# Centring two row tiles ahead of their 1/std at the start of a fused attention and MLP kernel

## The chip, the cores and the metric

The kernel runs on one core of a Trainium2 chip. The metric is the device time of a launch in microseconds, as a median over runs; the kernel before takes 693.07 us. The span in a profile is some 1.7 to 2.0 us shorter, as it goes from the first to the last instruction. Each run also records the mean clock granted to TensorE.

Names used below: PE is TensorE's matmul side, PEld its weight loads, DVE is VectorE, ACT is ScalarE, SP is the engine that issues nearly all DMAs. A *row tile* is 128 of the 2048 rows; block 0 is row tiles 0 to 3. V(j,c) is the group of eight matmuls that makes columns half c of V for row tile j. "Q" is the first of the 128 matmuls that make Q and K of block 0.

## The reference, cut to what matters

```python
def _layernorm(x, axis=-1, eps=1e-5):
    m = jnp.mean(x, axis=axis, keepdims=True)
    v = jnp.var(x, axis=axis, keepdims=True)
    return (x - m) / jnp.sqrt(v + eps)
...
    x = A_x                                              # 1 x 2048 x 1024, bf16
    h = x + _A_ref(_layernorm(x, axis=-1), A_wqkv, A_wo) # sliding window attention, 32 heads
    h2 = h + _B_ref(_layernorm(h, axis=-1), B_w1, B_w2)  # silu MLP, F = 3584
```

V = layernorm(x) @ Wv. Division by the standard deviation is one number for each row, so it can be done after the matmul: V = ((x - mean) @ Wv) * (1/std). The change uses this for two row tiles.

## The kernel before

Layernormed rows must lie transposed (features on partitions) in `lnT_b[0]` before TensorE can use them. Tiles 0, 1 and 2 of block 0 are transposed by TensorE and copied out of PSUM by ScalarE; tile 3 by a DMA transpose. In the traces VectorE, ScalarE and TensorE's matmuls run in the order in which the program issues them.

```python
    load_x(0, 0)
    load_wqkv(2 * D)              # V weights, columns half 0: 1 MB
    load_x(0, 1, nc.scalar)
    load_x(0, 2)
    load_wqkv(2 * D + 512)        # V weights, columns half 1: 1 MB
    load_x(0, 3)
    load_wqkv(0)                  # first 512 columns of Q
    ...
    for i in range(11):           # warm-up of TensorE
        nc.tensor.matmul(o_ps[i % 2][:]..., lhsT=warm[:, 0, 0:P], rhs=warm[:, 0, :], start=True, stop=True)

    def turn_first(j, h):         # two transposes by TensorE, one copy by ScalarE
        for i in range(2):
            kt = h * 2 + i
            nc.tensor.transpose(out=tp_ps[h][:, i * P:(i + 1) * P], in_=x_ring[j][:, kt * P:(kt + 1) * P], identity=ident[:])
        nc.scalar.copy(out=lnT_b[0][:, h * 2:(h + 1) * 2, j * P:(j + 1) * P], in_=tp_ps[h][:, 0:256]...)
    ...
    ln_stats(x_ring[0], st, 0)                 # bn_stats x2, bn_aggr
    ln_root(st, rs, 0)                         # ScalarE sqrt
    ln_half(x_ring[1], half, 0)
    ln_first(x_ring[0], st, rs, 0, 4, 1)       # reciprocal, (x - mean) * rstd in 4 pieces
    ln_stats(x_ring[1], st, 1, half)
    for h in range(4):
        turn_first(0, h)
        ...
    v_group(0, 0, 0, lambda **args: held.append(args), turn_1)
    ...
    v_group(0, 1, 0, act, turn_1_rest)
    ln_first(x_ring[2], st, rs, 2, 1)
    ln_stats(x_ring[3], st, 3)
    ln_root(st, rs, 3)
    ln_first(x_ring[3], st, rs, 3, 1)
    ln_transpose(x_ring[3], lnT_b[0], 3)       # DMA transpose
    for c0 in (D, 512, D + 512):
        load_wqkv(c0)
    v_group(0, 0, 1, act)
    for h in range(4):
        turn_first(2, h)
    v_group(0, 1, 1, act)
    v_group(0, 2, 0, act)
    ...                                        # V(2,1), V(3,0), V(3,1), then Q and K
```

The softmax here doesn't subtract the row's maximum and nothing guards it: scores larger than these inputs give would overflow.

Of the kernel before, what the change touches and what calls it, by code (L numbers as in the profile page):

```python
# [9 lines left out]
F32 = mybir.dt.float32  # L10
I32 = mybir.dt.int32
ACT = mybir.ActivationFunctionType
ALU = mybir.AluOpType

P = 128
# [29 lines left out]
def kernel(  # L45
# [10 lines left out]
    nc = tc.nc  # L56
# [3 lines left out]
    S, D = x2d.shape  # L60
# [4 lines left out]
    KT = D // P  # L65
# [4 lines left out]
    scale = float(DH) ** -0.5  # L70

    const = ctx.enter_context(tc.tile_pool(name="const", bufs=1))
    small = ctx.enter_context(tc.tile_pool(name="small", bufs=2))
# [12 lines left out]
    r_e = big.tile([P, 13312], BF16, name="r_e")  # L86
# [4 lines left out]
    tp_ps = [tp_pool.tile([P, 1024], BF16, name=f"tp{i}") for i in range(4)]  # L91
    o_ps = [ps.tile([P, 8, 64], F32, name=f"o_ps{i}") for i in range(2)]
    acc_ps = [ps.tile([P, 512], F32, name=f"acc{i}") for i in range(2)]

    def view(region, off, *dims):
        n = 1
        for d in dims:
            n *= d
        ap = region[:, off:off + n]
        if len(dims) == 2:  # L100
            return ap.rearrange("p (a b) -> p a b", b=dims[1])
        if len(dims) == 3:
            return ap.rearrange("p (a b c) -> p a b c", b=dims[1], c=dims[2])
        return ap
# [4 lines left out]
    lnT_b = [view(r_w, 24576, KT, 512), view(r_t, 0, KT, 512)]  # L109
    x_ring = [view(r_o, i * 1024, 1024) for i in range(8)]  # L110
# [17 lines left out]
    wqkv_v = A_wqkv.rearrange("(kt p) n -> p kt n", p=P)  # L128
# [5 lines left out]
    def load_x(b, j, queue=nc.sync):  # L134
        queue.dma_start(out=x_ring[(b % 2) * 4 + j], in_=x2d[(b * 4 + j) * P:(b * 4 + j + 1) * P, :])  # L135

    def load_wqkv(c0):
        dst = wqk[:, :, c0:c0 + 512] if c0 < 2 * D else wv[:, :, c0 - 2 * D:c0 - 2 * D + 512]
        nc.sync.dma_start(out=dst, in_=wqkv_v[:, :, c0:c0 + 512])

    eps = const.tile([P, 1], F32, name="eps")
    nc.vector.memset(eps[:], LN_EPS)
# [1 line left out]
    nc.scalar.activation(out=dummy[:], in_=eps[:], func=ACT.Sqrt)  # L144

    load_x(0, 0)
    load_wqkv(2 * D)
    load_x(0, 1, nc.scalar)
    load_x(0, 2)
    load_wqkv(2 * D + 512)  # L150
    load_x(0, 3)
    load_wqkv(0)

    ident = const.tile([P, P], BF16, name="ident")
    make_identity(nc, ident[:])
    warm = view(r_e, 0, 2, 512)
    nc.vector.memset(warm, 0.0)
    nc.gpsimd.memset(v[:, :, :, DH:VW], 1.0)


    for i in range(11):
        nc.tensor.matmul(o_ps[i % 2][:].rearrange("p a b -> p (a b)"), lhsT=warm[:, 0, 0:P], rhs=warm[:, 0, :], start=True, stop=True)


    def ln_half(xt, stats, c):
        nc.vector.bn_stats(out=stats[:, c, :], in_=xt[:, c * 512:(c + 1) * 512])

    def ln_stats(xt, st, j, half_done=None):
        stats = half_done
        if stats is None:  # L170
            stats = small.tile([P, 2, 6], F32, name="ln_st", tag="ln_st")
            ln_half(xt, stats, 0)
        ln_half(xt, stats, 1)
        nc.vector.bn_aggr(out=st[:, j, :], in_=stats[:])
# [18 lines left out]
    def ln_norm(xt, st, rs, j):  # L193
        nc.vector.tensor_scalar(out=xt, in0=xt, scalar1=st[:, j, 0:1], scalar2=rs[:, j:j + 1],
                                op0=ALU.subtract, op1=ALU.mult)

    def ln_transpose(xt, dst, j):
        nc.sync.dma_start_transpose(out=dst[:, :, j * P:(j + 1) * P], in_=xt)

    def ln_root(st, rs, j):  # L200
        nc.scalar.activation(out=rs[:, j:j + 1], in_=st[:, j, 1:2], func=ACT.Sqrt, bias=eps[:], scale=1.0)

    def ln_first(xt, st, rs, j, parts, on_act=0):

        if on_act:
            shift = small.tile([P, 2], F32, name="ln_shift", tag="ln_shift")
            nc.scalar.activation(out=shift[:, 0:1], in_=st[:, j, 0:1], func=ACT.Identity, scale=-1.0)
        nc.vector.reciprocal(out=rs[:, j:j + 1], in_=rs[:, j:j + 1])
        if on_act:
            nc.scalar.activation(out=shift[:, 1:2], in_=shift[:, 0:1], func=ACT.Identity, scale=rs[:, j:j + 1])  # L210
        n = 1024 // parts
        for h in range(parts):
            part = xt[:, h * n:(h + 1) * n]
            if h < parts - on_act:
                ln_norm(part, st, rs, j)
            else:
                nc.scalar.activation(out=part, in_=part, func=ACT.Identity, bias=shift[:, 1:2], scale=rs[:, j:j + 1])

    def turn_first(j, h):

        for i in range(2):
            kt = h * 2 + i
            nc.tensor.transpose(out=tp_ps[h][:, i * P:(i + 1) * P], in_=x_ring[j][:, kt * P:(kt + 1) * P], identity=ident[:])  # L223
        nc.scalar.copy(out=lnT_b[0][:, h * 2:(h + 1) * 2, j * P:(j + 1) * P],
                       in_=tp_ps[h][:, 0:256].rearrange("p (k q) -> p k q", q=P))

    def ln_tiles(tag):
        st = small.tile([P, 4, 2], F32, name=f"st_{tag}", tag=f"st_{tag}")
        rs = small.tile([P, 4], F32, name=f"rs_{tag}", tag=f"rs_{tag}")
        return st, rs  # L230
# [3 lines left out]
    acc_banks = list(a[:] for a in acc_ps)  # L234

    def next_acc():
        acc_n[0] += 1
        return acc_banks[acc_n[0] % len(acc_banks)]

    def v_group(b, j, c, copy, between=None):  # L240
        acc = next_acc()
        for kt in range(KT):
            if between:
                between(kt)
            nc.tensor.matmul(acc, lhsT=lnT_b[b % 2][:, kt, j * P:(j + 1) * P], rhs=wv[:, kt, c * 512:(c + 1) * 512],  # L245
                             start=(kt == 0), stop=(kt == KT - 1))
        copy(out=v[:, b * 4 + j, c * 16:(c + 1) * 16, 0:DH], in_=acc.rearrange("p (h d) -> p h d", d=DH))
# [172 lines left out]
    class Stream:  # L420
# [18 lines left out]
        def between(self, kt):  # L439
            if self.seen * self.n >= self.done * 192:  # L440
                self.bursts[self.done]()
                self.done += 1
            if self.seen * self.n * 2 >= (self.given * 2 + 1) * 192:
                if pending:
                    pending.pop(0)()
                coming.append(self.pieces[self.given])
                if len(coming) > self.behind:
                    pending.append(coming.pop(0))
                self.given += 1
            self.seen += 1  # L450

    dve, act = nc.vector.tensor_copy, nc.scalar.copy


    st, rs = ln_tiles("a")
    half = small.tile([P, 2, 6], F32, name="ln_st", tag="ln_st")
    ln_stats(x_ring[0], st, 0)
    ln_root(st, rs, 0)
    ln_half(x_ring[1], half, 0)
    ln_first(x_ring[0], st, rs, 0, 4, 1)  # L460
    ln_stats(x_ring[1], st, 1, half)
    for h in range(4):
        turn_first(0, h)
        if h == 2:
            ln_root(st, rs, 1)
    ln_first(x_ring[1], st, rs, 1, 4)
    ln_stats(x_ring[2], st, 2)

    held = []

    def turn_1(kt):
        if kt == 7:
            turn_first(1, 0)

    def turn_1_rest(kt):
        if kt == 2:
            turn_first(1, 3)
            act(**held.pop())
            ln_root(st, rs, 2)

    v_group(0, 0, 0, lambda **args: held.append(args), turn_1)
    turn_first(1, 1)
    turn_first(1, 2)
    v_group(0, 1, 0, act, turn_1_rest)
    ln_first(x_ring[2], st, rs, 2, 1)
    ln_stats(x_ring[3], st, 3)
    ln_root(st, rs, 3)
    ln_first(x_ring[3], st, rs, 3, 1)
    ln_transpose(x_ring[3], lnT_b[0], 3)
    for c0 in (D, 512, D + 512):  # L490
        load_wqkv(c0)
    v_group(0, 0, 1, act)
    for h in range(4):
        turn_first(2, h)
    v_group(0, 1, 1, act)
    v_group(0, 2, 0, act)
    v_group(0, 2, 1, act)
    nc.scalar.activation(out=dummy[:], in_=eps[:], func=ACT.Exp)
    v_group(0, 3, 0, act)
    v_group(0, 3, 1, act)  # L500

    ps_tp.__exit__(None, None, None)
    ps_sc = tc.tile_pool(name="ps_sc", bufs=1, space=bass.MemoryType.PSUM, reuse_waits="tile")
# [28 lines left out]
    for g0 in range(0, G, 4):  # L532
        for w in range(2):
            for g in range(g0, g0 + 4):
                qk_group(0, w, g, dve if g % 2 else act)
                n = g0 * 2 + w * 4 + g % 4
# [105 lines left out]
    for b in range(NB):  # L642
# [4 lines left out]
        for ft in range(FT):  # L647
# [8 lines left out]
            if b == 0 and 6 <= ft < 14:  # L656
                j, c = divmod(ft - 6, 2)
# [60 lines left out]
```

## Time and profile before

| | before |
|---|---|
| time, median of 3 | 693.07 us (692.89 to 693.12) |
| PE busy | 677.0 us, 98% of the span |
| first V matmul | 7.92 us |
| V(2,0) starts | 15.92 us (worked out in the prediction) |
| Q starts | 22.82 us |

TensorE is busy from start to end, so an instruction of another engine counts only where TensorE waits for it. The change concerns the first 23 us alone; from Q on the two programs are the same.

### The profile page before, as it was taken

What the parts mean: (1) busy time and instruction counts of PE and PEld (TensorE: products, weight loads), DVE (VectorE), ACT (ScalarE), POOL (GpSimd) and SP (SyncE); (2) the same over time, 40 slices, a digit from 0 to 9 for tenths busy, and PEclk for the clock granted to TensorE, in tenths of its full rate; (3) what the DMA queues carried; (4) which work ended last, traced back from release to release, by engine and by line L of the source; (5) the groups of instructions that cost most, each with busy time, mean ns of one, the idle gap of its engine ahead of it and who ended that gap; (6) DMA issues with size and microseconds to landing.
All of it is one profiled execution on the core that took longest, in us unless ns stands there. A gap on an engine that the chain in (4) does not pass through costs nothing.

```text
span 691.4 us, 14107 instructions
## 1 busy us (share of the span) xinstructions
PE 677.0 (98%) x5895; PEld 331.6 (48%) x6011; DVE 290.5 (42%) x609; ACT 241.8 (35%) x463; POOL 160.4 (23%) x295
## 2 busy tenths in 40 slices
PE   8999999999999999999999999999999999999998
PEld 3444455555555555544444444444444444444445
DVE  5267646744444439534315133343133251333111
ACT  5326666766666666421310033300133100233000
POOL 1007666656666666500000000000000000000000
PEclk9999999999999999999999999999999999999999
DMA  8732242136241889971023410022300024100110
GB/s 251 251 55 78 39 80 61 26 63 183 73 131 17 241 235 281 213 277 50 12 80 111 93 39 0 1 91 69 85 0 1 17 95 95 39 1 1 30 39 24
DMA packets 76463, 60.95 MB, mean 88 GB/s; under 512 B 50288, under 2 KB 60528, under 8 KB 76400
## 3 DMA queue, kind: packets, MB, share of 16 engines
q1 hardware_dynamic: 76256, 59.78, 32.0%
q8 instruction: 47, 0.77, 0.5%
q10 hardware_dynamic: 144, 0.26, 0.1%
q14 instruction: 16, 0.13, 0.1%
HBM read 39.85 MB, written 8.39 MB: 70 GB/s over the span
## 4 chain that ended last, share of the span: by engine, by line
PE 97%; issue 1%; DMA 1%; SPq 0%; DVE 0%
PE hacc L628 19%; PE hacc L665 17%; PE acc L255 16%; PE acc L665 10%; PE acc L628 9%; PE acc L245 8%; PE acc L276 7%; PE o_ps L388 5%; PE sc L308 3%; PE hacc L276 1%; DMA r_w<-in_A_wqkv_dram 1%; PE sc L360 1%; PE sc L334 1%; PE tp L223 0%; SPq L135 0%
## 5 line engine op out<-in xcount | busy, mean ns | idle before, releaser
L378 POOL TENSOR_SCALAR_AFFINE_SELECT r_e<-r_e 128x512 bf16<-128x512 bf16 (+1 forms) x288 | 157.4, 561 | 126.6 <-ACT r_e L368 62.7
L665 PEld LDWEIGHTS <-r_a 128*128 128x128 bf16 x952 | 90.9, 98 | 103.0
L628 PEld LDWEIGHTS <-r_w 128*128 128x128 bf16 x896 | 87.4, 98 | 105.0 <-issue 0.2
L665 PE MATMUL hacc<-r_a 128*128 128x512 bf16 (+2 forms) x607 | 121.8, 359 | 0.5
L628 PE MATMUL hacc<-r_e,r_w 128*128 128x512 bf16 x444 | 99.7, 379 | 0.5
L320 ACT ACTIVATE r_e<-sc 128x768 bf16<-128x768 f32 x96 | 78.2, 814 | 48.3 <-PE sc L308 47.6
L637 ACT ACTIVATE r_n<-hacc 128x512 f32<-128x512 f32 x30 | 17.9, 597 | 178.9 <-PE hacc L628 175.5
L665 PE MATMUL acc<-r_a 128*128 128x512 bf16 x329 | 73.5, 379 | 0.4
L255 PEld LDWEIGHTS <-r_w 128*128 128x128 bf16 x512 | 44.2, 97 | 46.1 <-issue 1.0
L255 PE MATMUL acc<-r_t,r_w 128*128 128x512 bf16 x233 | 60.3, 379 | 2.4 <-issue 1.7
L257 DVE CAST r_a<-acc 128x512 bf16<-128x512 f32 x56 | 38.6, 690 | 56.6 <-PE acc L255 43.8
L255 PE MATMUL acc<-r_w 128*128 128x512 bf16 x240 | 58.0, 379 | 1.5 <-issue 0.9
L388 PEld LDWEIGHTS <-r_e 128*128 128x128 bf16 x1440 | 47.4, 96 | 17.9
L276 PE MATMUL acc<-r_o,r_a 128*128 128x512 bf16 x188 | 49.5, 379 | 1.9 <-issue 1.3
L628 PE MATMUL acc<-r_e,r_w 128*128 128x512 bf16 x213 | 48.9, 379 | 0.3
L388 PE MATMUL o_ps<-r_a,r_e 128*128 128x33 bf16 x1440 | 48.1, 178 | 0.1
L321 ACT ACTIVATE r_e<-sc 128x256 bf16<-128x256 f32 x96 | 37.6, 392 | 0.0
L680 DVE SCALAR_TENSOR_TENSOR r_t<-hacc,r_t 128x512 bf16<-128x512 f32 (+2 forms) x22 | 14.0, 635 | 55.2 <-PE hacc L665 53.8
L680 DVE SCALAR_TENSOR_TENSOR r_t<-acc,r_t 128x512 bf16<-128x512 f32 x12 | 8.3, 692 | 64.2 <-PE acc L665 58.8
L638 DVE SCALAR_TENSOR_TENSOR r_a<-r_n,hacc 128x512 bf16<-128x512 f32 x30 | 20.6, 688 | 33.0 <-ACT r_n L637 33.0
L628 PE MATMUL hacc<-r_a,r_w 128*128 128x512 bf16 x139 | 32.6, 379 | 0.3
L276 PEld LDWEIGHTS <-r_a 128*128 128x128 bf16 x256 | 21.8, 97 | 22.3
(79 smaller groups left out, 532.5 us busy)
## 6 DMA issues: line engine op xcount, KB each, us to landing
r_w<-in_B_w_dram SPq DMA_DIRECT2D x8, 896.0 KB, 5.2
r_a<-in_B_w_dram SPq DMA_DIRECT2D x7, 1024.0 KB, 7.5
r_w<-in_A_wqkv_dram SPq DMA_DIRECT2D x6, 1024.0 KB, 9.3
h_dram<-r_t SPq DMA_DIRECT2D x16, 256.0 KB, 2.5
r_t<-h_dram SPq DMA_DIRECT2D x16, 256.0 KB, 2.9
out_dram<-r_t SPq DMA_DIRECT2D x31, 128.0 KB, 1.7
r_o<-in_A_x_dram SPq DMA_DIRECT2D x15, 256.0 KB, 4.2
r_e<-h_dram SPq DMA_DIRECT2D x3, 1024.0 KB, 5.7
```

The costliest lines, as they stand in the source:

```text
L245: nc.tensor.matmul(acc, lhsT=lnT_b[b % 2][:, kt, j * P:(j + 1) * P], rhs=wv[:, kt, c * 512:(c + 1) * 512], start=(kt == 0), stop=(kt == KT ...
L255: nc.tensor.matmul(acc, lhsT=wqk[:, kt, col0:col0 + P], rhs=lnT_b[b % 2][:, kt, :], start=(kt == 0), stop=(kt == KT - 1))
L257: copy(out=(qT, kT)[which][b][:, g, :], in_=acc)
L276: nc.tensor.matmul(acc, lhsT=qT[b][:, g, j * P:(j + 1) * P], rhs=wo[:, g, c * 512:(c + 1) * 512], start=(g == 0), stop=(g == G - 1))
L308: nc.tensor.matmul(sc[hh // 2][half * 64:half * 64 + 64, hh % 2, col:col + qb - qa], lhsT=kT[t // 4][r0:r0 + DH, g, k0:k0 + 64], rhs=qT[b] ...
L320: nc.scalar.activation(out=tri[:, :, :, 64:256], in_=both, func=ACT.Exp, scale=scale)
L321: nc.scalar.activation(out=e[:, 1024:1280].rearrange("p (h q) -> p h q", q=P), in_=bank[:, :, 192:320], func=ACT.Exp, scale=scale)
L378: nc.gpsimd.affine_select(out=dst, in_=src, pattern=[[0, n] for n in dst.shape[1:-1]] + [[sgn, P]], compare_op=ALU.is_ge if upper else ALU ...
L388: nc.tensor.matmul(o_ps[pair][:, qt * 2 + hh, 0:VW], lhsT=chunk_of(i, bank, piece, pair, hh), rhs=v[:, b * 4 + kt, g * 4 + pair * 2 + hh, ...
L628: nc.tensor.matmul(acc, lhsT=w1[:, kt, ft * P:(ft + 1) * P], rhs=ln2T[b][:, kt, :], start=(kt == 0), stop=(kt == KT - 1))
L665: nc.tensor.matmul(acc[:, 0:c1 - c0], lhsT=gT[:, ft, j * P:(j + 1) * P], rhs=w2[ft // 4][:, ft % 4, c0:c1], start=(ft == 0), stop=(ft == F ...
L680: nc.vector.scalar_tensor_tensor(out=t_out[j % 2][:, c0:c1], in0=acc[:, 0:c1 - c0], scalar=0.5, in1=t_in[j % 2][:, c0:c1], op0=ALU.mult, o ...
```

## The change

Its intent is to let TensorE start sooner. Before, tile 0 had to have its mean, variance, root and reciprocal before it could be transposed. Now only its mean is made (half of it by a sum on ScalarE), the tile is centred and transposed, and 1/std follows when V is taken out of PSUM. Tile 1's mean is a sum on ScalarE. The V weights come in quarters and halves, so that the first matmuls can start on the first quarter. Tiles 0 and 1 must still be normalized in full for Q and K, which is done later, with two more DMA transposes. The warm-up of TensorE has ten matmuls instead of eleven and starts sooner, as VectorE clears less memory for it. The diff, cut (of the calls in its last part only the new ones are shown; those that they replace stand above):

```diff
     load_x(0, 0)
-    load_wqkv(2 * D)
-    load_x(0, 1, nc.scalar)
+    load_x(0, 1)
+    load_wqkv(2 * D, 4, (0, 3))
     load_x(0, 2)
-    load_wqkv(2 * D + 512)
+    load_wqkv(2 * D, 4, (3, 4))
+    load_wqkv(2 * D + 512, 2)
     load_x(0, 3)
     load_wqkv(0)
...
-    for i in range(11):
...
+    for i in range(10):
...
+    def mean_first():
+        nc.scalar.activation(out=scrap[:, 0:512], in_=x_ring[0][:, 512:1024], func=ACT.Identity, scale=-1.0 / D, accum_out=mean[:, 0:1])
+        ln_half(x_ring[0], half, 0)
+        nc.vector.tensor_scalar(out=mean[:, 1:2], in0=half[:, 0, 1:2], scalar1=half[:, 0, 4:5], scalar2=-0.25, op0=ALU.add, op1=ALU.mult)
+        nc.scalar.activation(out=scrap, in_=x_ring[1], func=ACT.Identity, scale=-1.0 / D, accum_out=mean[:, 2:3])
...
+    def scaled(j):                      # evacuation of a held V group, times 1/std of tile j
+        args = held.pop(0)
+        nc.scalar.activation(func=ACT.Identity, scale=rs[:, j:j + 1], **args)
...
+    mean_first()
+    center(0)
+    center(1)
+    turn_first(0, 0, x_mid[0])
+    turn_first(0, 1, x_mid[0])
+    v_group(0, 0, 0, hold, place({1: (0, 2), 3: (0, 3), 5: (1, 0), 6: (1, 1), 7: (1, 2)}))
+    turn_first(1, 3, x_mid[1])
+    ln_stats(x_ring[2], st, 2)
+    ln_root(st, rs, 2)
+    ln_stats(x_ring[0], st, 0, half)
+    ln_root(st, rs, 0)
+    ln_recip(rs, 2)
+    ln_norm(x_ring[2], st, rs, 2)
+    ln_recip(rs, 0)
+    v_group(0, 1, 0, hold)
+    v_group(0, 0, 1, hold)
+    scaled(0)
     ln_stats(x_ring[3], st, 3)
     ln_root(st, rs, 3)
+    ln_stats(x_ring[1], st, 1)
+    ln_root(st, rs, 1)
+    ln_recip(rs, 3)
+    ln_norm(x_ring[3], st, rs, 3)
     ln_transpose(x_ring[3], lnT_b[0], 3)
+    ln_recip(rs, 1)
+    scaled(1)
+    scaled(0)
+    v_group(0, 1, 1, hold)
+    for h in range(4):
+        turn_first(2, h, x_ring[2])
+    scaled(1)
+    for j in range(2):
+        ln_norm(x_ring[j], st, rs, j)
+        ln_transpose(x_ring[j], lnT_b[0], j)
     for c0 in (D, 512, D + 512):
         load_wqkv(c0)
```

While the V stage runs, four PSUM banks rotate instead of two, so that held groups can stay.

More of the change, by code (lines that the diff above doesn't have):

```diff
@@ L135, in load_x, with load_wqkv @@
         queue.dma_start(out=x_ring[(b % 2) * 4 + j], in_=x2d[(b * 4 + j) * P:(b * 4 + j + 1) * P, :])
-    def load_wqkv(c0):
+    def load_wqkv(c0, parts=1, some=None):
         dst = wqk[:, :, c0:c0 + 512] if c0 < 2 * D else wv[:, :, c0 - 2 * D:c0 - 2 * D + 512]
-        nc.sync.dma_start(out=dst, in_=wqkv_v[:, :, c0:c0 + 512])
+        n = KT // parts
+        for k in range(0, KT, n)[slice(*some or (0, parts))]:
+            nc.sync.dma_start(out=dst[:, k:k + n, :], in_=wqkv_v[:, k:k + n, c0:c0 + 512])
+    warm = view(r_e, 0, P)
+    nc.vector.memset(warm, 0.0)
     eps = const.tile([P, 1], F32, name="eps")
@@ L155 @@
     make_identity(nc, ident[:])
-    warm = view(r_e, 0, 2, 512)
-    nc.vector.memset(warm, 0.0)
     nc.gpsimd.memset(v[:, :, :, DH:VW], 1.0)
-    for i in range(11):
-        nc.tensor.matmul(o_ps[i % 2][:].rearrange("p a b -> p (a b)"), lhsT=warm[:, 0, 0:P], rhs=warm[:, 0, :], start=True, stop=True)
+    wide = bass.AP(tensor=warm.tensor, offset=warm.offset, ap=[warm.ap[0], [0, 4], warm.ap[1]])
+    for i in range(10):
+        nc.tensor.matmul(o_ps[i % 2][:].rearrange("p (a c) b -> p a (c b)", c=2), lhsT=warm, rhs=wide, start=True, stop=True)
     def ln_half(xt, stats, c):
@@ L201, in ln_root, with ln_recip, turn_first @@
         nc.scalar.activation(out=rs[:, j:j + 1], in_=st[:, j, 1:2], func=ACT.Sqrt, bias=eps[:], scale=1.0)
-    def ln_first(xt, st, rs, j, parts, on_act=0):
-        if on_act:
-            shift = small.tile([P, 2], F32, name="ln_shift", tag="ln_shift")
-            nc.scalar.activation(out=shift[:, 0:1], in_=st[:, j, 0:1], func=ACT.Identity, scale=-1.0)
+    def ln_recip(rs, j):
         nc.vector.reciprocal(out=rs[:, j:j + 1], in_=rs[:, j:j + 1])
-        if on_act:
-            nc.scalar.activation(out=shift[:, 1:2], in_=shift[:, 0:1], func=ACT.Identity, scale=rs[:, j:j + 1])
-        n = 1024 // parts
-        for h in range(parts):
-            part = xt[:, h * n:(h + 1) * n]
-            if h < parts - on_act:
-                ln_norm(part, st, rs, j)
-            else:
-                nc.scalar.activation(out=part, in_=part, func=ACT.Identity, bias=shift[:, 1:2], scale=rs[:, j:j + 1])
-    def turn_first(j, h):
+    def turn_first(j, h, src):
         for i in range(2):
             kt = h * 2 + i
-            nc.tensor.transpose(out=tp_ps[h][:, i * P:(i + 1) * P], in_=x_ring[j][:, kt * P:(kt + 1) * P], identity=ident[:])
+            nc.tensor.transpose(out=tp_ps[h][:, i * P:(i + 1) * P], in_=src[:, kt * P:(kt + 1) * P], identity=ident[:])
         nc.scalar.copy(out=lnT_b[0][:, h * 2:(h + 1) * 2, j * P:(j + 1) * P],
@@ L455 @@
     st, rs = ln_tiles("a")
-    half = small.tile([P, 2, 6], F32, name="ln_st", tag="ln_st")
-    ln_stats(x_ring[0], st, 0)
-    ln_root(st, rs, 0)
-    ln_half(x_ring[1], half, 0)
-    ln_first(x_ring[0], st, rs, 0, 4, 1)
-    ln_stats(x_ring[1], st, 1, half)
-    for h in range(4):
-        turn_first(0, h)
-        if h == 2:
-            ln_root(st, rs, 1)
-    ln_first(x_ring[1], st, rs, 1, 4)
-    ln_stats(x_ring[2], st, 2)
-    held = []
-    def turn_1(kt):
-        if kt == 7:
-            turn_first(1, 0)
@@ L475, in turn_1_rest @@
-    def turn_1_rest(kt):
-        if kt == 2:
-            turn_first(1, 3)
-            act(**held.pop())
-            ln_root(st, rs, 2)
-    v_group(0, 0, 0, lambda **args: held.append(args), turn_1)
-    turn_first(1, 1)
-    turn_first(1, 2)
-    v_group(0, 1, 0, act, turn_1_rest)
-    ln_first(x_ring[2], st, rs, 2, 1)
+    x_mid = [view(r_e, 1024 + 1024 * j, 1024) for j in range(2)]
+    scrap = view(r_e, 3072, 1024)
+    mean = small.tile([P, 3], F32, name="mean")
+    half = small.tile([P, 2, 6], F32, name="ln_half")
@@ new lines, in mean_first, with center @@
+    def mean_first():
[3 more added lines that the diff above has]
+        nc.scalar.activation(out=scrap, in_=x_ring[1], func=ACT.Identity, scale=-1.0 / D, accum_out=mean[:, 2:3])
+    def center(j):
+        for h in range(4):
+            out, in0 = (x[j][:, h * 256:(h + 1) * 256] for x in (x_mid, x_ring))
+            if j == 0:
+                nc.vector.tensor_scalar(out=out, in0=in0, scalar1=mean[:, 0:1], scalar2=mean[:, 1:2], op0=ALU.add, op1=ALU.add)
+            else:
+                nc.vector.tensor_scalar(out=out, in0=in0, scalar1=mean[:, 2:3], scalar2=None, op0=ALU.add)
@@ new lines, with hold, place @@
+    held = []
+    def hold(**args):
+        held.append(args)
+    def scaled(j):
+        args = held.pop(0)
+        nc.scalar.activation(func=ACT.Identity, scale=rs[:, j:j + 1], **args)
+    def place(at):
+        return lambda kt: turn_first(*at[kt], x_mid[at[kt][0]]) if kt in at else None
+    acc_banks += [o[:].rearrange("p a b -> p (a b)") for o in o_ps]
+    mean_first()
[4 more added lines that the diff above has]
+    v_group(0, 0, 0, hold, place({1: (0, 2), 3: (0, 3), 5: (1, 0), 6: (1, 1), 7: (1, 2)}))
@@ L486 @@
+    turn_first(1, 3, x_mid[1])
+    ln_stats(x_ring[2], st, 2)
+    ln_root(st, rs, 2)
+    ln_stats(x_ring[0], st, 0, half)
+    ln_root(st, rs, 0)
+    ln_recip(rs, 2)
[4 more added lines that the diff above has]
+    scaled(0)
     ln_stats(x_ring[3], st, 3)
     ln_root(st, rs, 3)
-    ln_first(x_ring[3], st, rs, 3, 1)
+    ln_stats(x_ring[1], st, 1)
+    ln_root(st, rs, 1)
+    ln_recip(rs, 3)
+    ln_norm(x_ring[3], st, rs, 3)
@@ L489 @@
     ln_transpose(x_ring[3], lnT_b[0], 3)
+    ln_recip(rs, 1)
+    scaled(1)
+    scaled(0)
+    v_group(0, 1, 1, hold)
+    for h in range(4):
+        turn_first(2, h, x_ring[2])
[3 more added lines that the diff above has]
+        ln_transpose(x_ring[j], lnT_b[0], j)
     for c0 in (D, 512, D + 512):
         load_wqkv(c0)
-    v_group(0, 0, 1, act)
-    for h in range(4):
-        turn_first(2, h)
-    v_group(0, 1, 1, act)
     v_group(0, 2, 0, act)
@@ L500 @@
     v_group(0, 3, 1, act)
+    del acc_banks[2:]
     ps_tp.__exit__(None, None, None)
```

## The prediction

> **What bounds the kernel now.** I began with the page: PE is 98% busy and carries 97% of the chain that ended last. TensorE therefore sets the end, and a change to the start counts only by the time at which TensorE gets through it.
>
> The diff touches nothing after the V stage of block 0, so I next read the chain of waits over the first 51 us (start, duration, what):
>
> ```profile
> 1.26 6.61 DMA r_w<-in_A_wqkv_dram
> 7.88 0.04 issue
> 7.92 1.67 PE acc L245 x7
> ...
> 13.90 0.45 PE tp L223 x8
> 14.35 8.63 PE acc L245 x40
> 22.98 0.22 PE acc L255
> ```
>
> The first V matmul waits for its 1 MB of V weights (7.87 us). From there PE hardly stops until the Q groups (L255). The 40 matmuls are the five groups V(1,1), V(2,0), V(2,1), V(3,0), V(3,1), written (row tile, column half). One group is 8 x 8.63/40 = 1.73 us. The timeline gives the same run by its starts, 14.19, with the first Q matmul at 22.82, so V(2,0) starts at 14.19 + 1.73 = 15.92. Behind V(2,0) lie 32 matmuls, 6.90 us, up to Q. My measure of the change is when V(2,0) starts in it.
>
> The issues by window give what can feed it, in order of issue from 1.7 to 5.5 us (the last figure is us from issue to landing; the windows overlap, so each line is one transfer):
>
> ```profile
> r_o<-in_A_x_dram SPq DMA_DIRECT2D x1, 256.0 KB, 6.8
> ...
> r_w<-in_A_wqkv_dram SPq DMA_DIRECT2D x1, 1024.0 KB, 9.2
> ...
> r_o<-in_A_x_dram SPq DMA_DIRECT2D x1, 256.0 KB, 9.0
> ...
> r_w<-in_A_wqkv_dram SPq DMA_DIRECT2D x1, 1024.0 KB, 9.8
> ```
>
> With the issue times 1.72, 2.35, 3.29 and 5.43 these land at 8.5 (x tile 2), 11.55 (V half 1), 12.3 (x tile 3) and 15.2 us (Q). Tiles 0 and 1 land at 0.81 + 3.4 = 4.2 and 0.97 + 3.9 = 4.9. From 7.87 to 15.2 us 2.62 MB came: 358 GB/s, a full stream.
>
> VectorE's timeline shows what tile 3 costs once it is there:
>
> ```profile
> 12.67 1.28 DVE L166 BATCH_NORM_STATS2 ln_st<-r_o 128x6 f32<-128x512 bf16 x2
> 13.98 0.21 DVE L174 BATCH_NORM_AGGREGATE st_a<-ln_st 128x2 f32<-128x12 f32 x1
> 14.55 0.16 DVE L208 RECIPROCAL rs_a<-rs_a 128x1 f32<-128x1 f32 x1 [0.36 <-ACT rs_a L201]
> 14.75 0.55 DVE L194 TENSOR_SCALAR r_o<-r_o,st_a,rs_a 128x1024 bf16<-128x1024 bf16 x1
> ```
>
> From statistics to statistics is 1.31 + 0.13 = 1.44 us (elsewhere the next one starts 0.13 after an aggregate), a reciprocal to a norm 0.20, a norm to the next instruction 0.46.
>
> The groups kept apart by shape give ScalarE's prices (mean ns after the busy us):
>
> ```profile
> L342 ACT ACTIVATE r_e<-sc 128x1024 bf16<-128x1024 f32 x24 | 23.3, 1021 | 10.5 <-PE sc L334 10.5
> L257 ACT CAST r_a<-acc 128x512 bf16<-128x512 f32 x8 | 4.7, 585 | 21.2 <-PE acc L255 21.2
> L224 ACT COPY r_w<-tp 128x256 bf16<-128x256 bf16 x12 | 3.8, 375 | 1.2 <-PE tp L223 1.2
> L217 ACT ACTIVATE r_o<-r_o,ln_shift,rs_a 128x256 bf16<-128x256 bf16 x1 | 0.6, 601 | 0.0
> ```
>
> **What the Trainium skill says.** "TensorE: Matmul & The Clock Gate", in the section on the array's architecture (16 sub-arrays of 32x32), calls ScalarE and VectorE strict FIFO: an instruction that waits holds back all behind it. The trace agrees: both run this stage in program order, and the reciprocal above kept a ready VectorE idle for 0.36 us. "DMA: Bandwidth & Descriptors", Queues, rings and completion order, says that descriptors of one ring are consumed in order; the landings above are in order of issue. "ScalarE: Activation LUTs", What ACT_TABLE_LOAD costs, gives 93 ns for each pointer operand; here two of them took a 256 column operation from 375 to 601 ns, 113 each. The clock gate page's Part 1 says that an idle window of about 3.4 us halves TensorE's clock, and that as long a busy one restores it. The warm-up, 11 matmuls in 4.87 us (443 ns each), against 216 in the V stage shows the two rates; no idle stretch here shows the fall.
>
> **The change, part by part.**
>
> *Loads.* Before x tile 3 the queue carries the same bytes (x 0 to 2, both V halves); they are only cut finer, and x tile 1 moves off ScalarE's queue. At about 0.7 us per 256 KB the quarters of V half 0 land (estimates) near 5.6, 6.3 and 7.0, and the last, behind x tile 2, near 8.4. V half 1 stays at 11.55, x tile 3 at 12.3, Q at 15.2.
>
> *The start.* Removed before the first transpose: half of tile 0's statistics, aggregate, root, reciprocal, shift. What stays is one half's statistics on VectorE (4.25 to 4.89) beside a sum of the other on ScalarE (0.6 and an accumulator read that I put at 0.2), one small operation, and centring in four pieces. The first piece is ready near 5.45 instead of 6.84. ScalarE then sums the whole of tile 1, about 1.0 + 0.2 us, ahead of the first copy, so that copy runs at 6.1 (7.34 before) and V(0,0) starts near 6.5. Its last two k steps wait for the fourth quarter: it ends near 8.95, tile 1's last transposes at 9.05. V(1,0) takes until 10.8, V(0,1) until 12.5 (its second half needs 11.55 and starts at 11.65), V(1,1) until 14.3, tile 2's transposes until 14.7. The same work is done at 15.92 now: PE is 1.2 us ahead.
>
> *What V(2,0) waits for.* Tile 2's four copies from PSUM stand on ScalarE behind two scaled evacuations, V(1,0) by tile 1's 1/std and V(0,1). The first needs reciprocal 1, which on VectorE stands behind statistics 3, statistics 1, reciprocal 3 and norm 3. Tile 1's statistics are work that used to be done by 8.1 us; now they follow x tile 3. Added up from 12.35: statistics 3, 1.44, is 13.79; statistics 1, 1.31 to its aggregate and 0.13, is 15.23; reciprocal 3, 0.20, is 15.43; norm 3, 0.46, is 15.89; reciprocal 1, 0.16 and the step to ScalarE (0.24 from its start, as at 6.26 to 6.50), is 16.13. An evacuation with a pointer scale is 585 + 113 = 700 ns, 600 of it before the next one starts: two of them give 17.33. The copy to the first weight load took 0.40 at 7.34, so V(2,0) starts near 17.75.
>
> *Sum.* 17.75 - 15.92 = 1.8 us later, with PE idle for some 3.0 us from 14.7. The 1.2 us won ahead of it are spent in that wait.
>
> *Behind it.* Banks are free in time: four rotate, and the evacuations above release those that V(2,0), V(2,1) and V(3,0) reuse. The three DMA transposes issue from 15.9 (15.32 before), each some 1.4 us of queue; the third is issued by 20.2 and, at the 4.8 us that block 1's first one takes, lands by about 23.6, before Q at 17.75 + 6.9 = 24.65. Tile 3's lands near 19.1, needed at 21.2. K weights and the next x tiles slip by about 3.3 us. Block 1's first statistics then wait until about 33.7; VectorE's next eviction, due near 35.2, is hardly late, and PE needs its bank a group later. All of that is hidden.
>
> **The rivals.**
>
> *PE keeps its lead.* If x tile 3 landed some 2 us sooner, or ScalarE did not hold the copies, V(2,0) would start at 14.75: 1.2 us faster, 691.9. For it speak the start, which really is shortened, and the care of the order. Against it speaks the full stream: 0.2 us is about all that moving tile 1 can win. I give it one chance in ten.
>
> *The clock falls in the gap.* PE would have no V matmul from 14.3 to 17.75, about one window; tile 2's transposes lie inside it. If it falls, a window of 3.4 us at half rate costs at least 1.7 us more: 696.5. A window has no fixed phase, and the gap hardly covers a whole one: one in eight.
>
> *The DMA transposes become the bound.* If three in a row took longer than in block 1, Q would wait for tile 1's. For it: a serial queue. Against: a margin of 1 us over a pessimistic landing. It would add at most about 1 us, 695.8.
>
> *A cold start.* The shorter warm-up ends near 5.3 with small holes until 6.5, so V(0,0) might run at half rate. It would lose some 1.7 us where PE has 3.0 to give away: no effect.
>
> **Range and chances.** 693.07 + 1.8 is 694.9; I take 694.8, as x tile 3 may be a little early. The low end, 693.0, allows 1.8 us off in the chain of VectorE and ScalarE; the high end, 696.6, holds the fallen clock. 2% is 13.9 us, which no reading of a stage of 15 us gives: within 2% has 0.99.
>
> **What would show it.** Right: first V matmul near 6.5; a PE wait of about 3 us ahead of V(2,0), put down to ScalarE's copies; ScalarE waiting for the reciprocal at about 16.1; VectorE waiting for x tile 3 near 12.3; Q from 24.6; the same durations behind. Wrong: x tile 3 landing before 11, tile 1's statistics ahead of it, Q before 22.8, or 427 ns matmuls after the gap.

## The result, and the profile after

| | before | after |
|---|---|---|
| time, median | 693.1 us (692.89 to 693.26, 4 runs) | 696.09 us (695.0 to 697.29, 4 runs) |
| first V matmul | 7.92 us | 6.18 us |
| V(1,1) and tile 2's transposes done | 15.92 us | 14.86 us |
| V(2,0) starts | 15.92 us | 17.78 us |
| Q starts | 22.82 us | 24.70 us |

(14.86 is 14.41, where the eight transposes start, and 0.45 us, which eight take in the chain shown in the prediction. In the kernel before, tile 2's transposes come ahead of V(1,1), so both are done where V(2,0) starts.)

The change costs 0.4%: the ratio of the times is 1.0044, with a 95% interval of 1.0029 to 1.0059. Such a ratio is the mean time of one kernel's runs over that of the other's of the same rounds, so it is not quite the ratio of the medians. The four runs of the changed kernel fall into pairs: 695.0 and 695.01 with a clock of 1.000, 697.29 and 697.17 with a mean clock of 0.998. The trace is of the first run.

PE's timeline of the changed kernel (start, duration, what, and in brackets the idle time ahead of it and what ended it):

```profile
6.18 0.39 PE L237 MATMUL acc<-r_w 128*128 128x512 bf16 x1 [0.25 <-ACT r_w L216]
...
8.56 0.38 PE L237 MATMUL acc<-r_w 128*128 128x512 bf16 x1 [0.47 <-DMA r_w<-in_A_wqkv_dram]
...
12.69 1.89 PE L237 MATMUL acc<-r_w 128*128 128x512 bf16 x8
14.41 0.61 PE L215 MATMUL tp<-ident,r_o 128*128 128x128 bf16 x8
17.78 1.90 PE L237 MATMUL acc<-r_w 128*128 128x512 bf16 x8 [2.76 <-ACT r_w L216]
```

V starts 1.7 us sooner than before, waits half a microsecond for its fourth weight quarter, and arrives at tile 2's transposes (14.41) well ahead. Then TensorE stands for 2.76 us in front of V(2,0), for a copy of ScalarE (L216 is the copy out of PSUM in `turn_first`). Where ScalarE was is in the chain of waits:

```profile
5.32 7.16 DMA r_o<-in_A_x_dram
...
12.50 1.30 DVE ln_st L171 x2
...
14.03 1.16 DVE ln_st L171 x2
...
15.49 0.55 DVE r_o L199
16.03 0.08 DVE rs_a L209
...
16.20 1.27 ACT r_a L475 x2
17.46 0.27 ACT r_w L216
...
17.78 1.90 PE acc L237 x8
...
24.86 0.22 PE acc L247
```

This chain goes from x tile 3's landing (12.48) through its statistics, tile 1's statistics, the norm of tile 3 and tile 1's reciprocal (L209) to two scaled evacuations (L475), and only then to the copy that tile 2 needs. The chain before began with a weight load and then consisted of TensorE alone. Tile 2 itself had been normalized by 10.8 us. VectorE's timeline shows that it stood idle just ahead of this chain:

```profile
10.71 0.16 DVE L209 RECIPROCAL rs_a<-rs_a 128x1 f32<-128x1 f32 x1
12.50 1.29 DVE L171 BATCH_NORM_STATS2 ln_st<-r_o 128x6 f32<-128x512 bf16 x2 [1.64 <-DMA r_o<-in_A_x_dram]
```

For 1.64 us it waited for tile 3, though tile 1, whose statistics came next, had been there since about 4.3 us (ScalarE begins to sum it at 4.27).

### The profile page after: what moved, and what is told of

It is laid out like the page before. It is cut to its first block, busy times and chain, and to the rows that moved or that the text cites.

```text
span 693.2 us, 14121 instructions
## 1 busy us (share of the span) xinstructions
PE 676.5 (98%) x5894; PEld 331.5 (48%) x6010; DVE 290.7 (42%) x613; ACT 243.6 (35%) x464; POOL 160.4 (23%) x295
## 4 chain that ended last, share of the span: by engine, by line
PE 96%; issue 1%; DMA 1%; SPq 1%; DVE 1%; ACT 0%; ACTq 0%
PE hacc L650 18%; PE hacc L687 17%; PE acc L247 16%; PE acc L687 10%; PE acc L650 9%; PE acc L237 7%; PE acc L268 7%; PE o_ps L380 5%; PE sc L300 3%; PE hacc L268 1%; DMA r_o<-in_A_x_dram 1%; PE sc L352 1%; PE sc L326 1%; PE o_ps L237 0%; SPq L141 0%
```

## The experiments

The theory: V(2,0) is held by that chain, through the order of VectorE and of ScalarE; the upper pair of times is TensorE's clock, which falls in the gap. The rivals: the two more DMA transposes bound the stage; the upper pair is chance or comes from the start; the lead is lost elsewhere. All results were correct.

### The control

The changed kernel, unchanged.

> The changed kernel as it is, once more, as the control of its own spread. Its four runs so far fall into two pairs, 695.0 and 697.2, the second pair with a mean granted clock of 0.998. Theory (the clock falls in the gap ahead of V(2,0) in some runs): again two groups 2.2 us apart, the later one always with 0.998, the earlier one with 1.000, and the kernel before with one group near 693.1. Rival (the second pair was a disturbance of that chip or moment): one group only, near 695.0.

Measured: 695.43, 696.83, 697.11, 697.08 and 696.89, with clocks of 1.000, 0.997, 0.998, 0.998 and 0.998. The kernel before: 693.34 us as the median of 11 runs, of which one, at 695.52, also had 0.998, and one at 694.92 had not. The two groups are there again on this chip, and the clock tells which is which; but they are 1.4 to 1.7 us apart, not 2.2. The kernel before was not in one group, as expected: a lower clock has come once without the gap, and what lowered it there is not known. In the traced run, the first, PE waits as before:

```profile
18.31 1.90 PE L237 MATMUL acc<-r_w 128*128 128x512 bf16 x8 [2.77 <-ACT r_w L216]
```

### Filling the gap

```diff
+    for i in range(12):
+        nc.tensor.matmul(acc_banks[1], lhsT=warm, rhs=wide, start=True, stop=True)
     v_group(0, 2, 0, act)
```

> Twelve dummy matmuls of 512 columns on zeros between tile 2's transposes and V(2,0), into the bank that V(2,0) overwrites: 12 x 0.216 = 2.6 us of TensorE work inside the gap of 14.9 to 17.8 us; nothing else moves. Theory (the upper group is the clock falling in the gap): only the lower group is left, every run near 695.0 at 1.000. Rival (the upper group comes from the start, where the warm-up is shorter and ends in small holes): two groups as in the control. Third: if the fall is not tied to TensorE's work at all, two groups too. V(2,0) should still start at 17.8.

Measured: 694.69 to 695.84 in five runs, median 695.15, every clock 1.000.

```profile
14.88 0.61 PE L215 MATMUL tp<-ident,r_o 128*128 128x128 bf16 x8
15.32 2.75 PE L518 MATMUL acc<-r_e 128*128 128x512 bf16 x12
18.00 1.90 PE L237 MATMUL acc<-r_w 128*128 128x512 bf16 x8
```

The second line is the filling. V(2,0) starts at 18.00, within the 17.78 to 18.31 of the changed kernel's traces, but no run of five is in the upper group, against four of five in the control on the same chip. Useless work of TensorE saves time here, which of the causes named only the clock explains. The start was the same in both, so the rival that blamed it is out.

### A longer gap

Two idle operations ahead of tile 2's copies on ScalarE.

```diff
     scaled(0)
+    for i in range(2):
+        nc.scalar.activation(out=scrap, in_=x_mid[1], func=ACT.Identity, scale=1.0)
     v_group(0, 1, 1, hold)
```

> Two idle operations of 128x1024 on ScalarE (about 0.95 us each behind another) ahead of tile 2's copies, so that the gap grows from 2.9 to about 4.8 us; everything else stays. V(2,0) starts near 19.7. Theory (an idle stretch lets TensorE's clock fall, and the changed kernel's gap is at the edge of it): now the clock falls in every run, all with a mean clock of about 0.998; the V matmuls behind the gap take 427 ns each instead of 216 for 3.4 us or more, Q starts near 28.3 to 28.6 and the time is near 699 (695.2 + 1.9 + 2.0). Rival (the upper group has another cause than the length of the gap): 697.1 with a clock of 1.000 in some runs at least, 216 ns matmuls behind the gap, Q near 26.6.

Measured: 698.7, 699.13, 698.98 with 0.998, and 700.36 with 0.995. The fall is now in the trace. First PE's timeline:

```profile
14.73 0.61 PE L215 MATMUL tp<-ident,r_o 128*128 128x128 bf16 x8
19.89 3.52 PE L237 MATMUL acc<-r_w 128*128 128x512 bf16 x8 [4.55 <-ACT r_w L216]
23.25 3.62 PE L237 MATMUL o_ps<-r_w 128*128 128x512 bf16 x16
28.43 3.83 PE L247 MATMUL acc<-r_w 128*128 128x512 bf16 x16
```

and the stretches behind the gap (the length, each engine's busy time with its instructions, the granted clock, the DMAs' share, GB/s):

```profile
20.00:22.00 2.00, 2.00 (x5) 0.62 (x5) 0.00 (x0) 1.25 (x4) 0.00 (x0) 0.50 0.88 167
...
24.00:26.00 2.00, 2.00 (x11) 0.88 (x9) 0.00 (x0) 0.85 (x3) 0.00 (x0) 1.00 1.09 363
```

V(2,0) takes 3.52 us instead of 1.90, at a clock of 0.50; from about 23.2 on it runs at full speed. The clock's own record has one stretch of 0.5, 3.412 us long: 1.7 us lost. The clock fell in all four runs, as expected; the one at 0.995 lost about two such stretches by its clock, and its trace was not kept.

### Two more looks at the changed kernel

> The changed kernel once more for one look, to catch the upper group in a trace: five of its nine runs so far were in it. Theory: if the run comes near 697 with a clock of 0.998, the V matmuls behind the gap take 427 ns each instead of 216 for about 3.4 us or more and Q starts near 26.5 or later; V(2,0) still starts near 17.8. Rival (the clock falls elsewhere): Q at 24.7 and long matmuls in another place. If the run comes near 695, it tells nothing of this.

> The changed kernel for one more look, to catch the upper group in a trace (five of ten runs so far). If it comes near 697 with 0.998: 427 ns matmuls from V(2,0) at 17.8 on and Q near 26.8. If near 695: as before, Q near 24.7 to 25.2.

Measured: 695.37 and 695.04, both with 1.000, so neither caught the upper group. Of the changed kernel's eleven runs five lie at 695.0 to 695.4, and six at 696.8 to 697.3. The fall itself has thus been seen in a trace of the longer gap only; in the changed kernel it rests on the clock of each run and on the filling. (The two expectations miscount: six of nine and six of ten runs were in the upper group.)

One thing stays open. The four runs of the eleven of which a trace was kept (695.0, 695.43, 695.37 and 695.04) are all in the lower group, and six of the seven others in the upper. The record can't tell whether taking the trace has a part in it, so six in eleven is a count and not a rate. The filling stands without the traced runs too: none of its four others is in the upper group, against all four in the control.

### Tile 1's statistics first

```diff
     scaled(0)
-    ln_stats(x_ring[3], st, 3)
-    ln_root(st, rs, 3)
     ln_stats(x_ring[1], st, 1)
     ln_root(st, rs, 1)
-    ln_recip(rs, 3)
-    ln_norm(x_ring[3], st, rs, 3)
-    ln_transpose(x_ring[3], lnT_b[0], 3)
     ln_recip(rs, 1)
     scaled(1)
     scaled(0)
+    ln_stats(x_ring[3], st, 3)
+    ln_root(st, rs, 3)
+    ln_recip(rs, 3)
+    ln_norm(x_ring[3], st, rs, 3)
+    ln_transpose(x_ring[3], lnT_b[0], 3)
```

> Tile 1's statistics, root and reciprocal, and the two scaled evacuations, ahead of tile 3's statistics; VectorE idles there from 10.9 to 12.5 waiting for x tile 3, about the 1.44 us that they take. Theory (V(2,0) waits for the chain x tile 3, statistics 3, statistics 1, norm 3, reciprocal 1, evacuations, copies): the gap goes, V(2,0) starts near 15.0 instead of 17.8. Tile 3's DMA transpose is issued at 15.5 and lands at 19.0 where V(3,0) could start at 18.5, so that becomes the wait, and Q starts near 22.4: about 692.7, 0.4 below the kernel before, in one group. Rival (the extra DMA transposes bound the end of the stage): Q stays near 24.7 and the time near 695. Rival (TensorE's own order costs it): V(2,0) stays near 17.8.

Measured: 694.09 us (693.39 to 696.45, six runs), ratio to before 1.0011 (0.9995 to 1.0026), all clocks 1.000. V(2,0) starts at 15.28 and Q at 22.29 us, so the gap is gone and Q is 0.5 us sooner than before, as the theory said:

```profile
15.28 1.90 PE L237 MATMUL acc<-r_w 128*128 128x512 bf16 x8
...
22.29 4.05 PE L247 MATMUL acc<-r_w 128*128 128x512 bf16 x17
```

The two more DMA transposes are still there, so they were not what held Q at 24.7. The time is not sooner, since a wait came up behind Q (the trace is of the fastest of the six runs). PE's waits from 20 us on, then the chain:

```profile
PE acc L247 <- DVE r_a L249: 0.8, 1, 0.8
```

```profile
22.27 10.87 DMA r_o<-in_A_x_dram
33.16 1.30 DVE ln_st L171 x2
34.49 0.21 DVE st_a L179
34.69 0.56 DVE r_a L249
```

VectorE waits for the first x tile of block 1, does its statistics, and only then evicts the Q group whose bank TensorE needs. In the kernel before those loads start at 19.43, here at 22.27, behind three DMA transposes. I had called this wait hidden, and in the changed kernel it is; it comes out as soon as TensorE is on time.

### Block 1's x loads sooner

On top of the last one:

```diff
-    for c0 in (D, 512, D + 512):
-        load_wqkv(c0)
+    load_wqkv(D)
+    for j in range(4):
+        load_x(1, j)
+    load_wqkv(512)
+    load_wqkv(D + 512)
     ...
-    for j in range(4):
-        load_x(1, j)
```

> Tile 1's statistics first as before, and block 1's x loads put ahead of the two last Q and K weight loads. In the run with tile 1's statistics first Q started at 22.3, 0.5 sooner than in the kernel before, but PE waited 0.8 us for a VectorE eviction that stood behind statistics of block 1's first x tile, landing at 33.1. Theory (that late landing ate the gain, and its variation made that run's spread from 693.4 to 696.5): x lands near 28, the wait goes, the time is 692.5 with a spread under 0.5. Rival (the spread comes from TensorE's clock or the chip): spread as before, 693.4 to 696.5.

Measured: 693.1 us (692.68 to 693.31), ratio 0.9997 (0.9984 to 1.0009). The wait behind Q is gone. The spread is 0.6 us (under 0.5 was expected) where it was 3.1, but on another chip: there the kernel before spread over 2.5 us, here over 0.5. So that the late landing made the spread is not shown, and the rival that the chip made it is not out. The 692.5 was missed: in this trace the fourth V quarter came later (9.21, against 8.53 in the last one), V(2,0) started at 15.78, 0.5 us later, VectorE got to tile 3's statistics at 13.35 (12.69), V(3,0) waited 0.3 us for tile 3's DMA transpose, and Q started at 22.99.

### ScalarE's order alone

```diff
     ln_stats(x_ring[1], st, 1)
-    ln_root(st, rs, 1)
     ln_recip(rs, 3)
     ...
-    ln_recip(rs, 1)
-    scaled(1)
-    scaled(0)
     v_group(0, 1, 1, hold)
     for h in range(4):
         turn_first(2, h, x_ring[2])
+    ln_root(st, rs, 1)
+    ln_recip(rs, 1)
+    scaled(1)
+    scaled(0)
     scaled(1)
```

> Only ScalarE's order: tile 2's four copies ahead of root 1 and the scaled evacuations; VectorE's order, the loads and the DMA transposes stay. Theory (the copies wait because ScalarE runs in order behind reciprocal 1): V(2,0) starts near 15.1 instead of 17.8. Then V(2,1) needs the bank that the first scaled evacuation frees near 17.15, and V(3,0) needs tile 3's DMA transpose (16.06 + 3.5 = 19.6), so Q starts near 23.0 and the time is about 693.4, 1.7 below the changed kernel's lower group, in one group. Rival (VectorE, not ScalarE's order, holds tile 2): V(2,0) stays at 17.8 and the time at 695.

Measured: 694.43 us (694.09 to 695.39, four runs), ratio 1.0015 (1.0000 to 1.0031), all at 1.000. V(2,0) starts at 15.85, 0.3 us behind the transposes, so the order of ScalarE alone had held it, and the rival that tile 2 was held by VectorE is out:

```profile
15.11 0.61 PE L215 MATMUL tp<-ident,r_o 128*128 128x128 bf16 x8
15.85 1.90 PE L237 MATMUL acc<-r_w 128*128 128x512 bf16 x8
```

But the time is a microsecond above what I expected. The trace, of the slowest of the four runs, has Q waiting 0.5 us for a DMA transpose until 24.07 and later 1.05 us for the eviction behind block 1's x. Its third DMA transpose was issued only at 19.43 and took 4.5 us to land; the expectation had reckoned with 3.5 us for the first of the three and had left the third out.

### Tile 3's rows sooner

```diff
-    load_wqkv(2 * D + 512, 2)
+    load_wqkv(2 * D + 512, 2, (0, 1))
     load_x(0, 3)
+    load_wqkv(2 * D + 512, 2, (1, 2))
```

> Only the order of the loads: x tile 3 ahead of the second half of V half 1, so it lands about 1.45 us sooner, near 11.05, and that weight half near 12.5. Theory (the chain behind x tile 3 sets V(2,0)): V(2,0), Q and the end come 1.4 to 1.5 us sooner, Q at 23.25, 693.6; V(0,1) waits some 0.7 us for its weights, which is inside the gap and costs nothing, and with the gap down to about 1 us the upper group goes. Rival (ScalarE's evacuations or the DMA transposes set it, whatever x tile 3 does): 695.0, and two groups.

Measured: 693.56 us (693.5 to 694.2, five runs), every clock 1.000, ratio 1.0002 (0.9989 to 1.0014).

```profile
12.58 0.81 PE L238 MATMUL o_ps<-r_w 128*128 128x512 bf16 x3 [0.28 <-DMA r_w<-in_A_wqkv_dram]
...
16.33 1.90 PE L238 MATMUL acc<-r_w 128*128 128x512 bf16 x8 [0.56 <-ACT r_w L217]
...
23.25 2.97 PE L248 MATMUL acc<-r_w 128*128 128x512 bf16 x12
```

Nothing but the order of two loads differs (the lines are shifted by one). In the control on this chip VectorE began tile 3's statistics at 13.02, V(2,0) started at 18.31 and Q at 25.22, in 695.43 us; here these are 11.08, 16.33, 23.25 and 693.50. All four moved by 1.9 to 2.0 us (1.4 to 1.5 was expected). That is the 1.92 us for which VectorE had waited for x tile 3 in the control; here it does not wait for it at all. The chain does start at x tile 3.

### A version from the account, and one part undone in it

Tile 2's transposes and V(2,0) follow V(1,0) directly; ScalarE's copies stand ahead of the scaled evacuations; tile 3 is loaded sooner and block 1's x too.

```diff
     v_group(0, 1, 0, hold)
-    v_group(0, 0, 1, hold)
+    for h in range(4):
+        turn_first(2, h, x_ring[2])
     scaled(0)
     ln_stats(x_ring[3], st, 3)
     ln_root(st, rs, 3)
+    v_group(0, 2, 0, act)
     ...
     scaled(1)
+    v_group(0, 0, 1, hold)
     scaled(0)
     v_group(0, 1, 1, hold)
-    for h in range(4):
-        turn_first(2, h, x_ring[2])
     scaled(1)
     ...
-    v_group(0, 2, 0, act)
```

> The version that the account points to: tile 2's transposes and V(2,0) right behind V(1,0), while V half 1 still lands; copies ahead of the scaled evacuations; x tile 3 ahead of the second half of V half 1; block 1's x loads ahead of the last Q and K weights. Theory: no PE wait over 0.3 us after V(0,0); tile 3's transpose issued at 14.8, landed at 18.2, V(3,0) at 18.5, Q at 21.95, 0.87 sooner than in the kernel before: about 692.3 in one group. Rival (three DMA transposes now bound Q): T1 is issued near 17.6 and lands at 21.0; if it is late by more than 1 us, Q waits and the time is near 693. Rival (the earlier lead is lost again later, on loads): Q at 21.95 but a time of 693 or more.

> The version with tile 2 sooner as it was, on the same chip as the whole load, as its control and for a second estimate against the kernel before: 692.1 to 693.2, Q near 22.0 to 22.7 as the loads land. If it is faster than the kernel before by less than 1 us again, the stage has nothing more to give by order alone, since the x and V loads set it.

Measured: 692.95 us (692.06 to 693.62), and on another chip 692.52 (692.3 to 693.11); both ratios to before are 0.9993 (0.9981 to 1.0006). So it is about 0.5 us below the kernel before in both, which the intervals do not settle. Q starts at 22.70 and 22.72, 0.1 us sooner than before. TensorE loses its lead to the landing of the fourth V quarter (9.2 us, where the prediction had 8.4), as V(0,0) ends near 9.8; behind that it hardly waits. None of the readings of the first expectation held in full: Q was not at 21.95. The range of the second held; that order alone has nothing more to give, as it concludes, was not tested.

The last experiment undoes the cut loads in this version.

```diff
-    load_x(0, 1)
-    load_wqkv(2 * D, 4, (0, 3))
+    load_wqkv(2 * D)
+    load_x(0, 1, nc.scalar)
     load_x(0, 2)
-    load_wqkv(2 * D, 4, (3, 4))
```

> The version with tile 2 sooner, with one part of the change undone: V half 0 in one load of 1 MB behind x tile 0, x tile 1 from ScalarE's queue, x tile 2 behind, as in the kernel before. V half 0 then lands whole near 7.9, and V(0,0) runs from there to about 9.9 with its transposes; in the cut version it started at 6.1 but waited twice for quarters and its last two matmuls came at 9.2 to 9.9. Theory (the stream and not the cutting sets the end of V(0,0)): V(2,0) and Q within 0.3 us of the cut version, Q at 22.4 to 23.0, the time 692.6 to 693.2. Rival (the cut loads are what makes the sooner start worth something): V(0,0) ends 1 us later, Q at 23.7, 693.9.

Measured: 694.82 us (694.38 to 696.19), 2.3 us above its control on the same chip. Both readings failed (Q starts at 25.81 in the trace). The trace, of the slowest of the five runs, says why in that run:

```profile
5.29 0.63 PE L215 MATMUL tp<-ident,r_e 128*128 128x128 bf16 x4
7.75 0.58 PE L237 MATMUL acc<-r_w 128*128 128x512 bf16 x1 [1.82 <-DMA r_w<-in_A_wqkv_dram]
...
8.35 1.06 PE L237 MATMUL acc<-r_w 128*128 128x512 bf16 x2
```

The weights landed at 7.7 us, as expected, but two matmuls now take 1.06 us in place of 0.59: TensorE runs at half clock, until 13.56 by the clock's own record, which its matmuls bear out. Between the warm-up's end at 5.5 and 7.75 it had only four transposes to do. The two versions differ in these loads alone, so in these traces the shorter warm-up is enough only with the matmuls that the first quarters put right behind it. What the cut loads are worth without this, the run can't tell. (The four untraced runs, at 694.38 to 694.84, are faster than the traced one. Three of them have a clock of 0.998 and the traced one 1.000, since its record begins with the first rise; that the three rose and fell again in the hole is only argued.)

## Why the prediction was right

**The chain to V(2,0)** was right in every link: x tile 3 landed at 12.48 (12.3 predicted), reciprocal 1 started at 15.95 (15.89), the first scaled evacuation at 16.20 (16.13), the first copy at 17.35 (17.33), V(2,0) at 17.78 (17.75) and Q at 24.70 (24.65). That the end agrees to 0.05 us is in part luck: tile 3's statistics began 0.15 us late (12.50 for 12.35), and the terms behind them were 0.12 us too long in sum. In the three other traces of the changed kernel they begin at 12.73 to 13.02, and V(2,0) starts at 18.01 to 18.31. The experiments on VectorE's order, on ScalarE's order and on tile 3's load each removed or shortened one link, and V(2,0) came 3.0, 2.4 and 2.0 us sooner than in the changed kernel's trace on the same chip (18.31, 18.23 and again 18.31).

**The start** was right in size. Tile 0 landed at 3.5 instead of 4.2; of these 0.7 us V gained 0.3 (6.18 and not 6.5), as the transposes at 5.29 follow directly on the warm-up. The fourth V quarter then held V(0,0) for half a microsecond. With tile 2's transposes done at 14.86 against 14.7, the lead over before was 1.1 us, all of it lost in the wait. The cold start cost nothing, as said: in the changed kernel's four traces at most the first V matmul was slow (0.59 us instead of 0.39).

**Behind V(2,0)** the banks and the DMA transposes were hidden, as said; the third transpose was issued at 19.0 and took at most 3.5 us, so it was there by 22.5 at the latest. (The 23.6 predicted for it is 4.8 us from the start of its issue, 18.8, and not from the 20.2 that stands beside it.) Block 1's x landed at 34.0 against 33.7, and no PE wait came of it. "All of that is hidden" holds for the changed kernel only: with TensorE on time, it became the next wait.

**The clock** was the term that was mis-sized. I named the fall, its place and its price (at least 1.7 us), but put it at one in eight, as "the gap hardly covers a whole one". The lower clock came in six runs of eleven. The clock records of the kept traces show what it turns on. In all ten traces that have one, the time from the clock's first rise to its next change is a whole multiple of 3.413 us (four times it in the longer gap; 200 to 202 times in the others, where that change comes after the program's end), and the first rise comes at 3.9 to 6.8 us from the start, or at 13.56 in the whole load. So the clock is set on a grid of 3.413 us, whose place differs from run to run.

In the longer gap the window from 16.38 to 19.80 us was wholly idle, and the clock fell at its end. In the control's traced run, which kept its clock, the grid has a boundary at 16.32, which cuts the 2.77 us of waiting into 0.8 and 2.0. In the changed kernel's four traces TensorE stands for 2.46 to 2.77 us, less than a window. If the gaps of the runs that fell were like these, a window that is mostly empty is enough, and the place of the grid decides. This last step is only argued, as none of those runs has a trace.

The two groups are why the median is 696.09, between them, where no run lies, and not the 695.0 of the lower group, which lies 0.2 us from the 694.8 predicted.

**Chances and range**: within 2%, as given 0.99, and inside 693.0 to 696.6. That the median lies inside is in part luck, since two of the four runs fell and two did not: the upper runs, near 697, lie just outside, and so does the control's median of 696.89, with four of five runs in the upper group. The high end took the smallest price of a fall. One of the signs of being wrong, 427 ns matmuls after the gap, must by the clock have come up in the six upper runs, though no trace shows it there.

**The rival that was given one chance in ten**, PE keeping its lead, was what the experiments then built: with the gap gone the kernel is level with the one before, or 0.5 us below it, not the 1.2 us of that rival, because the next waits stand close behind.

## What to carry to other kernels

When work is taken off the start of a chain, look where it is put down: tile 1's statistics went behind a tile that lands late, and an in-order engine made other, ready work wait for them. Let an engine do what is there before it waits for what is not, and issue the copies on which TensorE depends ahead of evacuations that only free a bank. A TensorE gap of about 3 us can cost more than its length, by the clock, and in only some of the runs, so look at each run's clock before trusting a median, and do not take the traced runs to stand for all.

## What the Trainium skill lacked or had wrong

- "TensorE: Matmul & The Clock Gate", Part 1, says that the clock falls after at least one idle window of about 3.4 us. The stretch of half clock recorded here was 3.412 us, which agrees. But how empty a window has to be is lacking: a gap of 3.37 us (14.41 to 17.78) with 0.45 us of transposes in it went with the lower clock in six runs of eleven, one of 5.2 us (14.73 to 19.89) in four of four, and one of 1.2 us (15.17 to 16.33) in none of five; a window with 2.0 us of waiting in it (the control's trace) kept the clock.
- The same page gives about 3.4 us of work as the warm-up. In the whole load's trace 4.45 us of warm-up matmuls, with 0.63 us of transposes next and then nothing until 7.75, left the matmuls at 427 ns until 13.56. On that run's grid the windows that ended at 6.73 and 10.15 had 0.8 and 1.0 us without work in them and did not raise the clock; in the run with tile 3's rows sooner a window with 0.57 us (0.48 to 3.89, the warm-up starting at 1.05) did. How full a window must be to raise the clock is lacking as well.
- In the profile the granted clock reads 1.00 during the warm-up, where the matmuls take 443 ns each: there is no record ahead of the first change, and four kept traces (the changed kernel's first, its two more looks, and block 1's x loads sooner) have none at all. So a mean of 1.000 does not by itself show that the clock was full throughout. The same page warns that clock events can be unreliable, but not of this; matmul durations have to be read instead.
- "ScalarE: Activation LUTs", What ACT_TABLE_LOAD costs, has the price of an operation and of its pointer operands (an evacuation went from 0.59 to 0.69 us with one pointer, which agrees with its 93 ns). It lacks that an accumulator output is a further instruction of its own, of 0.19 us here, behind each of the two sums.
